# Column norms by a matmul with ones, and V taken group by group, in the attention phase of a fused kernel on one core

## The chip, the cores and the metric

The kernel runs on one core of a Trainium2 chip. The metric is the device time of one execution in microseconds (us). The kernel before takes 2712.07 us (median of 6 runs, 2706.3 to 2716.43).

## The reference

Two blocks follow each other. The first is a cross-covariance attention: the attention matrix is only 256 x 256, taken over the channels, and the sum runs over 5696 tokens. The second mixes tokens with two 5696 x 5696 matrices and channels with a 256 x 256 one. There are 4 batches.

```python
# q, k, v: (4, 5696, 256)
qn = q / (np.linalg.norm(q, axis=1, keepdims=True) + 1e-06)   # norm over the tokens, per channel
kn = k / (np.linalg.norm(k, axis=1, keepdims=True) + 1e-06)
a = softmax(kn.transpose(0, 2, 1) @ qn / tau)                 # (4, 256, 256), rows
x = v @ a
theta = x @ w_theta
zr, zi = x * np.cos(theta), x * np.sin(theta)
y = einsum('ts,bsd->btd', w_tok_r, zr) + einsum('ts,bsd->btd', w_tok_i, zi)
u = x + y
out = u + np.maximum(u @ w_ch, 0.0)
```

## The kernel before

Tokens are cut into 45 chunks of 128 rows (the last has 64), and the chunks into 12 groups of four (the last group is the 64-row chunk alone). The program has three parts. Phase 1 does the attention and the phases cos and sin for each of the 4 batches and leaves zr in SBUF, x and zi in DRAM. Pass 0 multiplies w_tok_r with zr, pass 1 w_tok_i with zi and finishes the output. The change touches phase 1 alone.

Phase 1 runs over the batches in a Python loop, and a batch has four stages, each in PSUM pools of its own that are opened and closed with the stage.

- **Stream** (L113 to L195): for each group POOL issues loads of q, k and v (qb, kb, vb; L131, L138), which turn float32 into bfloat16 on the way, into pools of two buffers. For each chunk TensorE does six matmuls of 256 columns: two halves each of G = k^T q (L149), Gq = q^T q (L156) and Gk = k^T k (L163). They add up in PSUM over the 45 chunks. Of Gq and Gk only the diagonals are used: they are the squared norms. Then TensorE transposes v (stgv, L175) and VectorE copies the result to vT (L181), which holds the whole batch.
- **Softmax** (L197 to L261): the diagonals are taken out by multiplying with an identity and adding up (L204, L213), ScalarE takes square roots (L226), VectorE adds 1e-6 and takes reciprocals (L228). The column scale is spread over the partitions by a matmul of a diagonal matrix with ones (bc_ps, L236). Then s_h (L240), the row maximum (L251), exp on ScalarE (L255), its sum's reciprocal, and a_bf (L261).
- **xT** (L263 to L281): for the whole batch, x transposed = a_bf^T vT in pieces of 512 columns (xt_ps, L274; two PSUM buffers), copied by VectorE to xT (L281).
- **E** (L283 to L376): for each group, theta (th_ps, L302) and x (x_ps, L310), each four chunks wide and with two PSUM buffers. ScalarE takes cos (L323) and sin (L326) of th_ps and copies x (L329), 1024 columns at a time; VectorE multiplies zr (L330) and zi (L336); SP stores x and zi (L366).

"The x stage" below stands for xT and E together, written x(b) for batch b, and stream(b) for its stream. The order of the work within an engine's queue is chosen by the framework's scheduler from the order of the program, the dependences and the free buffers. An engine works through its queue in order. A buffer of a pool is given out again when its last reader is done; pools that share memory or PSUM wait for each other.

Passes 0 and 1 load a row panel of the matrix (Wb, L460), transpose it on TensorE (stg, L428), copy it out (wtev, L438) and multiply it with zr or zi (acc, L571).

Of the kernel before, what the change touches and what calls it, by code (L numbers as in the profile page):

```python
# [10 lines left out]
F32 = mybir.dt.float32  # L11
# [8 lines left out]
def _csz(S: int, P: int, j: int) -> int:  # L20
    return min(P, S - j * P)
# [3 lines left out]
def kernel(  # L25
# [12 lines left out]
    nc = tc.nc  # L38
# [50 lines left out]

    with ExitStack() as ph1:  # L90
        vtp = ph1.enter_context(tc.tile_pool(name="vtp", bufs=1))
        xtp = ph1.enter_context(tc.tile_pool(name="xtp", bufs=1))
        attn = ph1.enter_context(tc.tile_pool(name="attn", bufs=1))
# [4 lines left out]
        for b in range(B):  # L98
            pair = b // 2
            bcol = (b % 2) * D  # L100

            vT = vtp.tile([P, CH, S], BF16, name="vT")
            a_bf = attn.tile([P, CH, C], BF16, name="a_bf")

            with ExitStack() as esA:
                psA = esA.enter_context(
                    tc.tile_pool(name=f"psA{b}", bufs=1, space=bass.MemoryType.PSUM)
                )
                G_ps = psA.tile([P, CH, 512], F32, name="G_ps")
                Gq_ps = psA.tile([P, CH, 512], F32, name="Gq_ps")  # L110
                Gk_ps = psA.tile([P, CH, 512], F32, name="Gk_ps")

                with ExitStack() as esB:  # L113
                    psB = esB.enter_context(
                        tc.tile_pool(name=f"psB{b}", bufs=2, space=bass.MemoryType.PSUM)
                    )
                    for g in range(NG):
                        j0 = g * GRP
                        nchunks = min(GRP, NT - j0)
                        rows0 = j0 * P  # L120
                        rows1 = min(S, rows0 + nchunks * P)
                        grows = rows1 - rows0
                        nfull = grows // P
                        tail = grows - nfull * P

                        qb = cst.tile([P, GRP, C], BF16, name="qb")
                        kb = cst.tile([P, GRP, C], BF16, name="kb")
                        vb = cst.tile([P, GRP, C], BF16, name="vb")
                        for src, dst in ((q, qb), (k, kb), (v, vb)):
                            if nfull > 0:  # L130
                                nc.gpsimd.dma_start(  # L131
                                    dst[:, 0:nfull, :],
                                    src[b, rows0:rows0 + nfull * P, :].rearrange(
                                        "(j p) c -> p j c", p=P
                                    ),
                                )
                            if tail > 0:
                                nc.gpsimd.dma_start(  # L138
                                    dst[0:tail, nfull, :],
                                    src[b, rows0 + nfull * P:rows1, :],  # L140
                                )

                        for r in range(nchunks):
                            j = j0 + r
                            csz = _csz(S, P, j)
                            first = j == 0
                            last = j == NT - 1
                            for h in range(CH):
                                nc.tensor.matmul(  # L149
                                    G_ps[:, h, 0:C],  # L150
                                    kb[0:csz, r, h * P:(h + 1) * P],
                                    qb[0:csz, r, :],
                                    start=first,
                                    stop=last,
                                )
                                nc.tensor.matmul(  # L156
                                    Gq_ps[:, h, 0:C],
                                    qb[0:csz, r, h * P:(h + 1) * P],
                                    qb[0:csz, r, :],
                                    start=first,  # L160
                                    stop=last,
                                )
                                nc.tensor.matmul(  # L163
                                    Gk_ps[:, h, 0:C],
                                    kb[0:csz, r, h * P:(h + 1) * P],
                                    kb[0:csz, r, :],
                                    start=first,
                                    stop=last,
                                )

                        for h in range(CH):
                            stgv = psB.tile([P, GRP, P], BF16, name="stgv")
                            for r in range(nchunks):
                                csz = _csz(S, P, j0 + r)
                                nc.tensor.transpose(  # L175
                                    stgv[:, r, 0:csz],
                                    vb[0:csz, r, h * P:(h + 1) * P],
                                    ident_bf[0:csz, 0:csz],
                                )
                            if tail == 0:  # L180
                                nc.vector.tensor_copy(  # L181
                                    vT[:, h, rows0:rows1],
                                    stgv[:, 0:nchunks, :].rearrange("p j n -> p (j n)"),
                                )
                            else:
                                if nfull > 0:
                                    nc.vector.tensor_copy(
                                        vT[:, h, rows0:rows0 + nfull * P],
                                        stgv[:, 0:nfull, :].rearrange("p j n -> p (j n)"),
                                    )  # L190
                                nc.vector.tensor_copy(
                                    vT[:, h, rows0 + nfull * P:rows1],
                                    stgv[:, nfull, 0:tail],
                                )

                with ExitStack() as esC:
                    psC = esC.enter_context(  # L197
                        tc.tile_pool(name=f"psC{b}", bufs=1, space=bass.MemoryType.PSUM)
                    )
                    dq = attn.tile([P, CH], F32, name="dq")  # L200
                    dk = attn.tile([P, CH], F32, name="dk")
                    scr = attn.tile([P, P], F32, name="scr")
                    for h in range(CH):
                        nc.vector.scalar_tensor_tensor(  # L204
                            out=scr,
                            in0=Gq_ps[:, h, h * P:(h + 1) * P],
                            scalar=1.0,
                            in1=ident_f32,
                            op0=MULT,
                            op1=MULT,  # L210
                            accum_out=dq[:, h:h + 1],
                        )
                        nc.vector.scalar_tensor_tensor(  # L213
                            out=scr,
                            in0=Gk_ps[:, h, h * P:(h + 1) * P],
                            scalar=1.0,
                            in1=ident_f32,
                            op0=MULT,
                            op1=MULT,
                            accum_out=dk[:, h:h + 1],  # L220
                        )
                    rq_col = attn.tile([P, CH], F32, name="rq_col")
                    rk_col = attn.tile([P, CH], F32, name="rk_col")
                    for src_c, dst_c, which in ((dq, rq_col, 0), (dk, rk_col, 1)):
                        srt = attn.tile([P, CH], F32, name="srt", tag=f"srt{which}")
                        nc.scalar.activation(srt, src_c, ACT.Sqrt)  # L226
                        nc.vector.tensor_scalar_add(srt, srt, 1e-6)
                        nc.vector.reciprocal(dst_c, srt)  # L228
# [9 lines left out]
                    for h in range(CH):  # L238
# [9 lines left out]
                        if inv_tau != 1.0:  # L248
                            nc.vector.tensor_scalar_mul(s_h, s_h, inv_tau)
# [372 lines left out]
```

## Time and profile before

| | |
|---|---|
| median of 6 runs | 2712.07 us |
| time of the profiled execution | 2714.03 us |
| its span (first to last instruction) | 2712.3 us |
| mean granted TensorE clock | 0.966 |
| TensorE busy, share of the span | 2411.6 us, 89% |
| VectorE | 598.2 us, 22% |
| ScalarE | 487.5 us, 18% |
| GpSimd (POOL) | 153.5 us, 6% |
| DMA moved | 260.89 MB, mean 96 GB/s |
| first matmul of pass 0 into acc | 503.94 us from the start |

Busy times overlap, and they are averages over parts of the program that have different limits: in the page's slices the busy share of TensorE is six to seven tenths in the first fifth of the span and nine tenths or more in most of the rest. What the change can be worth has to be read in phase 1, the first 504 us. PEld is the load of weights into TensorE; it overlaps the matmuls. The page's GB/s count what lands, that is bfloat16 bytes for the loads of q, k and v.

### The profile page before, as it was taken

Reading aid. Unit: us, or ns where it says so; the run is one execution under the profiler, and the core shown is the slowest. Engines: PE = TensorE matmul, PEld = TensorE weight load, DVE = VectorE, ACT = ScalarE, POOL = GpSimd, SP = SyncE. Lnnn points to the kernel's source line nnn. Section 1 sums busy time; section 2 is a strip of 40 time slices with the busy share of each in tenths; the row PEclk is TensorE's granted clock in tenths of the full one; section 3 lists DMA queues with packets and bytes.
Section 4 is the critical chain, followed back from the end, with each engine's and each line's share of the span. In section 5 each row is a group of like instructions: output and inputs, shape, how many; then the busy total and the mean of one; then the engine's idle time right before and its main releaser. Section 6 shows DMA issues by size and latency. Waiting matters only on the chain.

```text
span 2712.3 us, 34757 instructions
## 1 busy us (share of the span) xinstructions
PE 2411.6 (89%) x14985; PEld 1294.8 (48%) x15238; DVE 598.2 (22%) x1390; ACT 487.5 (18%) x795; POOL 153.5 (6%) x242
## 2 busy tenths in 40 slices
PE   6766676699999999999999669999999999999998
PEld 4445454344444444444444334445444444444454
DVE  2433424111111111111111102222221222222122
ACT  0505143211111111111111001111111111111111
POOL 4031220000000000000000000000000000000000
PEclk9978888899999999999999889999999999999999
DMA  9486684544444444444443454433433443344331
GB/s 154 112 112 133 85 156 83 120 89 89 89 89 88 89 88 89 88 89 88 86 84 83 109 148 99 100 79 89 100 86 84 98 100 84 84 101 99 76 92 40
DMA packets 231322, 260.89 MB, mean 96 GB/s; under 512 B 8320, under 2 KB 214144, under 8 KB 219776
## 3 DMA queue, kind: packets, MB, share of 16 engines
q0 software_dynamic: 83488, 164.79, 35.4%
q1 hardware_dynamic: 147680, 93.87, 11.3%
q8 instruction: 119, 1.95, 0.3%
q14 instruction: 35, 0.29, 0.0%
HBM read 365.07 MB, written 58.33 MB: 156 GB/s over the span
## 4 chain that ended last, share of the span: by engine, by line
PE 74%; issue 15%; DVE 4%; POOL 2%; DMA 2%; SPq 1%; ACT 1%; DVEq 0%; POOLq 0%; ACTq 0%
PE acc L571 64%; PE stg L428 8%; PE g_ps L521 2%; DVE u L497 1%; DVE utev L514 1%; POOL vb L131 1%; POOL qb L131 1%; DVE wtev L438 1%; DMA zi_dram<-zi 1%; SPq L411 1%; POOL kb L131 1%; DMA zi_res<-zi_dram 0%; DMA kb<-in_k_dram 0%; SPq L484 0%; PE xt_ps L274 0%
## 5 line engine op out<-in xcount | busy, mean ns | idle before, releaser
L571 PEld LDWEIGHTS <-wtev 128*128 128x128 bf16 (+1 forms) x8100 | 745.9, 98 | 808.8 <-issue 44.5
L571 PE MATMUL acc<-zi_res,wtev 128*128 128x512 bf16 (+2 forms) x3919 | 942.5, 380 | 45.0 <-DMA zi_res<-zi_dram 37.9
L571 PE MATMUL acc<-zr_res,wtev 128*128 128x512 bf16 (+2 forms) x3932 | 943.0, 380 | 6.8 <-DVE wtev L453 0.4
L438 ACT COPY wtev<-stg 128x512 bf16<-128x512 bf16 x440 | 257.9, 586 | 1343.8 <-PE stg L428 1296.1
L438 DVE COPY wtev<-stg 128x512 bf16<-128x512 bf16 x528 | 222.7, 422 | 1254.5 <-PE stg L428 1202.1
L428 PEld LDWEIGHTS <-Wb 128*128 128x128 bf16 (+2 forms) x4050 | 297.0, 98 | 278.8 <-issue 111.9
L428 PE MATMUL stg<-ident_bf,Wb 128*128 128x128 bf16 (+2 forms) x4050 | 389.5, 220 | 41.2 <-DVE wtev L438 22.4
L149 PE MATMUL G_ps<-qb,kb 128*128 128x256 bf16 x360 | 113.6, 315 | 65.2 <-DMA kb<-in_k_dram 55.1
L156 PE MATMUL Gq_ps<-qb 128*128 128x256 bf16 x360 | 113.1, 315 | 7.0 <-DMA qb<-in_q_dram 7.0
L478 DVE TENSOR_TENSOR up<-acc,x_in 128x512 bf16<-128x512 f32 (+1 forms) x90 | 61.7, 686 | 240.9 <-PE acc L571 240.9
L163 PE MATMUL Gk_ps<-kb 128*128 128x256 bf16 x360 | 113.1, 314 | 0.0
L497 DVE TENSOR_TENSOR u<-acc,up_in 128x512 f32<-128x512 f32 (+1 forms) x90 | 58.1, 686 | 243.4 <-PE acc L571 237.9
L302 PE MATMUL th_ps<-wth,xT 128*128 128x256 bf16 x360 | 50.9, 272 | 43.3 <-ACT sin_t L326 40.5
L521 PE MATMUL g_ps<-wch,utev 128*128 128x256 bf16 (+1 forms) x360 | 47.1, 274 | 47.3 <-DVE utev L514 47.3
L460 POOL DMA_DIRECT2D Wb<-in_moe_w_tok_i_dram x45 | 23.8, 529 | 1140.1 <-PE stg L428 1113.9
L504 ACT CAST u4b<-u 128x1024 bf16<-128x1024 f32 (+1 forms) x45 | 47.0, 1045 | 220.2 <-DVE u L497 220.2
L460 POOL DMA_DIRECT2D Wb<-in_moe_w_tok_r_dram x45 | 23.8, 530 | 1040.0 <-PE stg L428 976.7
L274 PE MATMUL xt_ps<-vT,a_bf 128*128 128x512 bf16 (+1 forms) x188 | 57.5, 404 | 25.2 <-DVE a_bf L261 16.3
L181 DVE COPY vT<-stgv 128x512 bf16<-128x512 bf16 x88 | 33.3, 420 | 197.6 <-PE stgv L175 197.6
L149 PEld LDWEIGHTS <-kb 128*128 128x128 bf16 x360 | 40.2, 112 | 70.1 <-DMA kb<-in_k_dram 60.1
L448 ACT COPY wtev<-stg 64x128 bf16<-64x128 bf16 x88 | 22.8, 259 | 282.4 <-PE stg L428 282.4
L530 DVE SCALAR_TENSOR_TENSOR or<-g_ps,u 128x256 f32<-128x256 f32 (+1 forms) x180 | 63.8, 418 | 17.4 <-PE g_ps L521 17.4
(71 smaller groups left out, 856.0 us busy)
## 6 DMA issues: line engine op xcount, KB each, us to landing
Wb<-in_moe_w_tok_r_dram POOLq DMA_DIRECT2D x44, 1424.0 KB, 10.9
Wb<-in_moe_w_tok_i_dram POOLq DMA_DIRECT2D x44, 1424.0 KB, 10.1
out_dram<-or SPq DMA_DIRECT2D x44, 512.0 KB, 4.6
qb<-in_q_dram POOLq DMA_DIRECT2D x44, 256.0 KB, 5.0
kb<-in_k_dram POOLq DMA_DIRECT2D x44, 256.0 KB, 6.0
vb<-in_v_dram POOLq DMA_DIRECT2D x44, 256.0 KB, 6.7
x_dram<-x SPq DMA_DIRECT2D x44, 256.0 KB, 2.3
zi_dram<-zi SPq DMA_DIRECT2D x44, 256.0 KB, 2.3
```

The costliest lines, as they stand in the source:

```text
L131: nc.gpsimd.dma_start(dst[:, 0:nfull, :], src[b, rows0:rows0 + nfull * P, :].rearrange("(j p) c -> p j c", p=P),)
L149: nc.tensor.matmul(G_ps[:, h, 0:C], kb[0:csz, r, h * P:(h + 1) * P], qb[0:csz, r, :], start=first, stop=last,)
L156: nc.tensor.matmul(Gq_ps[:, h, 0:C], qb[0:csz, r, h * P:(h + 1) * P], qb[0:csz, r, :], start=first, stop=last,)
L163: nc.tensor.matmul(Gk_ps[:, h, 0:C], kb[0:csz, r, h * P:(h + 1) * P], kb[0:csz, r, :], start=first, stop=last,)
L274: nc.tensor.matmul(xt_ps[:, 0:ncol], a_bf[:, h, hp * P:(hp + 1) * P], vT[:, h, t0:t0 + ncol], start=(h == 0), stop=(h == CH - 1),)
L428: nc.tensor.transpose(stg[0:ssz, r, 0:prows], Wb[0:prows, j * P:j * P + ssz], ident_bf[0:prows, 0:prows],)
L438: cp(wtev[:, 0:nchunks, :].rearrange("p j n -> p (j n)"), stg[:, 0:nchunks, :].rearrange("p j n -> p (j n)"),)
L478: nc.vector.tensor_tensor(up4[0:prows, 2 * qq:2 * qq + 2, :].rearrange("p b d -> p (b d)"), acc[qq][0:prows, :], x_in[0:prows, 2 * qq:2 * ...
L497: nc.vector.tensor_tensor(u4[0:prows, 2 * qq:2 * qq + 2, :].rearrange("p b d -> p (b d)"), acc[qq][0:prows, :], up_in[0:prows, 2 * qq:2 * ...
L521: nc.tensor.matmul(gq[bb // 2][0:prows, bb % 2, :], utev[:, bb * CH + h, 0:prows], wch[:, h, :], start=(h == 0), stop=(h == CH - 1),)
L530: nc.vector.scalar_tensor_tensor(out=or4[0:prows, bb, :], in0=gq[bb // 2][0:prows, bb % 2, :], scalar=0.0, in1=u4[0:prows, bb, :], op0=MAX ...
L571: nc.tensor.matmul(acc[qq][0:prows, :], wtev[0:ssz, r, 0:prows], zpairs[qq][0:ssz, j, :], start=(j == 0), stop=(j == NT - 1),)
```

## The change

Phase 1 is written anew as three functions that the batch loop calls one after the other: stream(b), softmax and xstage(b). All their pools are opened once for the whole phase.

- The norms: VectorE squares qb and kb into sq (bfloat16, 512 columns a chunk), and TensorE multiplies sq with a matrix of ones into nrm_ps, 512 columns wide. Every partition then holds the squared norms of all columns of q and k. Gq, Gk, the diagonal matrices and bc_ps go; ScalarE takes the root of nrm_ps's q half directly (bcq), and VectorE takes its reciprocal, now on 128 x 256 elements. The k half is still brought to one value a partition with the identity.
- stream(b) loads q and k only, with four buffers each.
- xstage(b) loads v itself, group by group (four buffers), transposes a group (stgv, now both halves in one tile, one PSUM buffer), copies it out in one step of 1024 columns, makes xT of that group (xt_ps, two PSUM buffers), and then th_ps and x_ps for two chunks at a time, with one PSUM buffer each. The steps of ScalarE and VectorE on them are 512 columns wide. vT and xT of a whole batch are no longer kept.
- PSUM: G_ps two banks, nrm_ps one, stgv one, xt_ps two, th_ps one, x_ps one.

The core of the diff:

```diff
-        vtp = ph1.enter_context(tc.tile_pool(name="vtp", bufs=1))
-        xtp = ph1.enter_context(tc.tile_pool(name="xtp", bufs=1))
-        cst = ph1.enter_context(tc.tile_pool(name="cst", bufs=2))
+        cst = ph1.enter_context(tc.tile_pool(name="cst", bufs=4))
+        vr = ph1.enter_context(tc.tile_pool(name="vr", bufs=4))
+        tg = ph1.enter_context(tc.tile_pool(name="tg", bufs=2))
...
+        psA = ph1.enter_context(tc.tile_pool(name="psA", bufs=1, space=bass.MemoryType.PSUM))
+        psX = ph1.enter_context(tc.tile_pool(name="psX", bufs=1, space=bass.MemoryType.PSUM))
+
+        def stream(b: int):
...
+                for src, dst in ((q, qb), (k, kb)):
...
+                sq = cst.tile([P, GRP, 2 * C], BF16, name="sq")
+                    nc.vector.tensor_tensor(
+                        sq[:, 0:nfull, 0:C], qb[:, 0:nfull, :], qb[:, 0:nfull, :], MULT
+                    )
...
+                    nc.tensor.matmul(
+                        nrm_ps[:, 0:2 * C],
+                        ones_bf[0:csz, :],
+                        sq[0:csz, r, :],
+                        start=first,
+                        stop=last,
+                    )
...
+        def softmax(G_ps, nrm_ps):
+            nc.scalar.activation(bcq, nrm_ps[:, 0:C], ACT.Sqrt)
...
+            nc.vector.reciprocal(bcq, bcq)
...
+        def xstage(b: int, a_bf):
...
+                vb = vr.tile([P, GRP, C], BF16, name="vb")
+                stgv = psX.tile([P, CH, GRP, P], BF16, name="stgv")
+                vT_g = tg.tile([P, CH, GRP * P], BF16, name="vT_g")
...
+                xT_g = tg.tile([P, CH, GRP * P], BF16, name="xT_g")
+                    xt_ps = psX.tile([P, GRP * P], F32, name="xt_ps", bufs=2)
...
+                for pr0 in range(0, nchunks, 2):
+                    th_ps = psX.tile([P, 2, D], F32, name="th_ps")
+                    x_ps = psX.tile([P, 2, D], F32, name="x_ps")
...
+        for b in range(B):
+            G_ps, nrm_ps = stream(b)
+            a_bf = softmax(G_ps, nrm_ps)
+            xstage(b, a_bf)
```

The order of the instructions on the engines at three places. First TensorE, in the x stage of the first batch. Before, xt of the whole batch comes first, then th and x:

```order
L274 MATMUL xt_ps<-vT,a_bf 128x64
L302 LDWEIGHTS xT
L302 MATMUL th_ps<-wth,xT 128x256
L302 LDWEIGHTS xT
L302 MATMUL th_ps<-wth,xT 128x256
L310 LDWEIGHTS vT
L310 MATMUL x_ps<-a_bf,vT 128x256
```

After, a little behind the beginning of x(0) (L153 and L160 belong to stream(1), the other lines to x(0)):

```order
L153 LDWEIGHTS kb
L153 MATMUL G_ps<-qb,kb 128x256
L160 LDWEIGHTS ones_bf
L160 MATMUL nrm_ps<-sq,ones_bf 128x512
L153 LDWEIGHTS kb
L153 MATMUL G_ps<-qb,kb 128x256
L293 LDWEIGHTS xT_g
L293 MATMUL th_ps<-wth,xT_g 128x256
L268 LDWEIGHTS a_bf
L268 MATMUL xt_ps<-vT_g,a_bf 128x512
L301 LDWEIGHTS vT_g
L301 MATMUL x_ps<-a_bf,vT_g 128x256
```

The matmuls of stream(b+1) stand between those of x(b): from the first xt of x(0) to its last th, the chunks 12 to 34 of the 45 of stream(1); the first 11 stand ahead of it, in the softmax of batch 0, and the last 11 behind it. In the steady part a pair's four th are followed by four x of the next pair, then by xt, or by transposes and one chunk of the stream.

Second VectorE, in the softmax of the first batch. Before:

```order
L213 SCALAR_TENSOR_TENSOR scr,dk<-Gk_ps,ident_f_66 128x128
L227 TENSOR_SCALAR srt<-srt 128x2 x2
L228 RECIPROCAL rq_col<-srt 128x2
L228 RECIPROCAL rk_col<-srt 128x2
L232 TENSOR_SCALAR diagm<-ident_f_66,rq_col 128x128
L237 COPY bc_sb<-bc_ps 128x128
L232 TENSOR_SCALAR diagm<-ident_f_66,rq_col 128x128
L237 COPY bc_sb<-bc_ps 128x128
L240 SCALAR_TENSOR_TENSOR s_h<-G_ps,rk_col,bc_sb 128x256 x2
```

After (sq here is that of stream(1), vT_g that of x(0)):

```order
L134 TENSOR_TENSOR sq<-qb 128x4x256
L247 COPY vT_g<-stgv 128x1024
L137 TENSOR_TENSOR sq<-kb 128x4x256
L175 SCALAR_TENSOR_TENSOR scr,dk<-nrm_ps,ident_f_66 128x128
L185 TENSOR_SCALAR bcq<-bcq 128x256
L175 SCALAR_TENSOR_TENSOR scr,dk<-nrm_ps,ident_f_66 128x128
L186 RECIPROCAL bcq<-bcq 128x256
L188 TENSOR_SCALAR dk<-dk 128x2
L247 COPY vT_g<-stgv 128x1024
L189 RECIPROCAL rk_col<-dk 128x2
L134 TENSOR_TENSOR sq<-qb 128x4x256
L193 SCALAR_TENSOR_TENSOR s_h<-G_ps,rk_col,bcq 128x256 x2
```

Squares of the next stream's groups now stand among the softmax steps: those of its first two groups ahead of the first step, those of its third and fourth ahead of s_h, exp's sum and a_bf.

Third POOL, at the end of phase 1. Before, the panels of pass 0 follow the last loads:

```order
L131 DMA qb<-in_q_dram 128x4x256
L131 DMA kb<-in_k_dram 128x4x256
L131 DMA vb<-in_v_dram 128x4x256
L138 DMA qb<-in_q_dram 64x256
L138 DMA kb<-in_k_dram 64x256
L138 DMA vb<-in_v_dram 64x256
L460 DMA Wb<-in_moe_w_tok_r_dram 128x5696 x44
```

After:

```order
L229 DMA vb<-in_v_dram 128x4x256 x4
L121 DMA qb<-in_q_dram 128x4x256
L121 DMA kb<-in_k_dram 128x4x256
L128 DMA qb<-in_q_dram 64x256
L128 DMA kb<-in_k_dram 64x256
L452 DMA Wb<-in_moe_w_tok_r_dram 128x5696
L229 DMA vb<-in_v_dram 128x4x256 x3
L452 DMA Wb<-in_moe_w_tok_r_dram 128x5696
L229 DMA vb<-in_v_dram 128x4x256 x4
L234 DMA vb<-in_v_dram 64x256
L452 DMA Wb<-in_moe_w_tok_r_dram 128x5696 x42
```

The first two panels of pass 0 are issued ahead of the last eight loads of v, and on TensorE the transposes of the first panel stand at the beginning of x(3). From the second panel on the passes hold the same instructions in the same order as before.

More of the change, by code (lines that the diff above doesn't have):

```diff
@@ L222 @@
[L222 to L228, printed above, removed]
@@ L305 @@
+                                th_ps[0:csz, rr, :],
+                                xT_g[:, h, r * P:r * P + csz],
                                 wth[:, h, :],
```

433 lines of the change are left out of this document (200 added, 233 removed).

## The prediction

> **What bounds the kernel now.** The page first: where the time lies.
>
> ```profile
> span 2712.3 us, 34757 instructions
> PE 74%; issue 15%; DVE 4%; POOL 2%; DMA 2%; SPq 1%; ACT 1%; DVEq 0%; POOLq 0%; ACTq 0%
> ```
>
> The profiled execution took 2714.0 us round this span, 2 us above the median of the runs shown (2712.07). From the first acc matmul on, TensorE is dense; the change doesn't touch that code. So the timeline: where do the stages begin?
>
> ```profile
> 8.49 0.39 PE L149 MATMUL G_ps<-qb,kb 128*128 128x256 bf16 x1 [0.63 <-DMA kb<-in_k_dram]
> 60.41 0.29 DVE L204 SCALAR_TENSOR_TENSOR scr<-Gq_ps,ident_f 128x128 f32<-128x128 f32 x1 [0.19 <-PE Gk_ps L163]
> 69.57 8.17 PE L274 MATMUL xt_ps<-vT,a_bf 128*128 128x512 bf16 x23 [4.07 <-DVE a_bf L261]
> 190.65 0.61 PE L274 MATMUL xt_ps<-vT,a_bf 128*128 128x512 bf16 x1 [4.07 <-DVE a_bf L261]
> 503.94 2.58 PE L571 MATMUL acc<-zr_res,wtev 128*128 128x512 bf16 x7 [0.22 <-issue]
> ```
>
> Phase 1 lasts 504 us: stream to 60, softmax 9 us, then the x stage, and a batch comes every 121 us (69.57 to 190.65). The stretches of the first batch (stream, softmax, xT, E), and the handover to pass 0:
>
> ```profile
> 0.00:61.00 61.00, 39.83 (x360) 32.73 (x360) 10.90 (x32) 1.28 (x1) 28.94 (x47) 0.97 1.14 153
> 61.00:70.00 9.00, 1.99 (x6) 1.27 (x8) 5.89 (x28) 2.78 (x7) 2.90 (x4) 0.56 1.27 167
> 70.00:90.00 20.00, 16.93 (x78) 7.49 (x77) 14.82 (x24) 2.94 (x3) 0.00 (x0) 0.94 0.03 4
> 90.00:123.00 33.00, 19.98 (x159) 15.56 (x157) 14.62 (x24) 32.70 (x36) 0.00 (x0) 0.96 0.54 169
> 487.00:504.00 17.00, 1.66 (x13) 1.47 (x15) 0.95 (x4) 0.59 (x1) 0.00 (x0) 0.50 0.95 213
> ```
>
> The columns are PE, PEld, DVE, ACT, POOL, granted clock, DMA share and GB/s. Each stretch has another limit: the stream the loads, xT VectorE and TensorE, E ScalarE (32.7 of 33 us), the handover the DMA queues; while one is limited the rest idle. The waits of the phase say the same:
>
> ```profile
> POOL qb L131 <- PE Gk_ps L163: 290.3, 36, 64.0
> PE G_ps L149 <- DMA kb<-in_k_dram: 55.1, 26, 4.1
> 9.00:10.00 1.00, 1.00 (x7) 0.67 (x6) 0.00 (x0) 0.00 (x0) 0.00 (x0) 1.00 1.45 196
> 13.00:14.00 1.00, 1.00 (x12) 0.90 (x10) 0.10 (x1) 0.00 (x0) 1.00 (x3) 1.00 0.56 48
> ```
>
> Loads wait up to 64 us for a buffer, a whole x stage. The full rate is 196 GB/s (at 9 us), with holes (48 GB/s at 13 us) until two buffers come free, hence 153 over the stream.
>
> **The change part by part.** The order of the instructions is given with the change: of the 45 chunks of stream(b+1) 23 now stand between the matmuls of x(b), 11 ahead of them in softmax. So a period is not a sum of stages any more, but the larger of a dependency chain and the busiest engine. The durations:
>
> ```profile
> 450.46 0.38 PE L310 MATMUL x_ps<-a_bf,vT 128*128 128x256 bf16 x2
> 450.68 0.38 PE L302 MATMUL th_ps<-wth,xT 128*128 128x256 bf16 x2
> 508.53 1.89 PE L571 MATMUL acc<-zr_res,wtev 128*128 128x512 bf16 x8
> 20.61 0.54 PEld L175 LDWEIGHTS <-vb 128*128 128x128 bf16 x8
> 459.10 1.16 ACT L323 ACTIVATE cos_t<-th_ps,pio 128x1024 bf16<-128x1024 f32 x1
> 462.00 1.19 ACT L323 ACTIVATE cos_t<-th_ps,pio 128x1024 bf16<-128x1024 f32 x1
> L438 ACT COPY wtev<-stg 128x512 bf16<-128x512 bf16 x440 | 257.9, 586 | 1343.8 <-PE stg L428 1296.1
> 456.35 0.69 DVE L330 TENSOR_TENSOR zr_res<-x,cos_t 128x1024 bf16<-128x1024 bf16 x1 [6.16 <-ACT x L329]
> 456.96 0.68 DVE L336 TENSOR_TENSOR zi<-x,sin_t 128x1024 bf16<-128x1024 bf16 x1
> 442.50 7.69 DVE L281 CAST xT<-xt_ps 128x512 bf16<-128x512 f32 x12 [0.55 <-PE xt_ps L274]
> 21.14 0.75 DVE L181 COPY vT<-stgv 128x512 bf16<-128x512 bf16 x2 [4.89 <-PE stgv L175]
> ```
>
> *TensorE.* Gq, Gk (4 matmuls of 256 columns a chunk) and the small bc matmuls go; one nrm matmul of 512 columns comes. 256 columns cost 0.107 us (two in 0.22), 512 cost 0.216 ((1.89 - 0.38)/7), a transpose 0.068 (8 in 0.54). A batch after: G 90 x 0.107 = 9.6, nrm 45 x 0.216 = 9.7, transposes 90 x 0.068 = 6.1, xt 46 x 0.216 = 9.9, th and x 180 x 0.107 = 19.3: 55 us.
>
> *ScalarE.* The ops are halved to 512 columns: three of 1024 start 2.90 us apart, 0.97 each; a 512 one lies between half of that (0.48) and the 0.586 of the copy; I take 0.54. 66.75 of them are 36 us, with softmax and table loads 42.
>
> *VectorE.* zr/zi of 1024 take 0.61 (456.35 to 456.96), of 512 between 0.31 and that: 0.37, 44 of them 16.3; casts 0.64 (7.69/12), 22 are 14; vT copies of 1024 at most two of 512, 0.75, 8.3; new: sq, 22.25 of 1024 at 0.65, 14.5; softmax some 5. Together 58 us. Of these, sq stands in the queue before the softmax steps and has to wait for its loads.
>
> *DMA.* Bytes don't change. One load (256 KB) takes 1.34 us at 196 GB/s; a batch has 33.4: 44.7 us. Its stores, 5.8 MB, move at 169 GB/s with share 0.54, so take 18.6 us of the engines. Together 63 us. Four buffers in place of two should close the holes. POOL's queue takes v loads in between now, but its issuing is no limit: 28.94 us in the first stretch for more than a batch of loads.
>
> No engine needs more than 63 us of the 121 now spent. Now the chain, with the rows of the hand-over between engines:
>
> ```profile
> 465.90 1.21 ACT L326 ACTIVATE sin_t<-th_ps,zerob 128x1024 bf16<-128x1024 f32 x1
> 467.17 1.03 PE L302 MATMUL th_ps<-wth,xT 128*128 128x256 bf16 x8 [0.99 <-ACT sin_t L326]
> L260 DVE RECIPROCAL rinv<-ssum 128x1 f32<-128x1 f32 x8 | 1.3, 164 | 0.3
> L261 DVE TENSOR_SCALAR a_bf<-e_h,rinv 128x256 bf16<-128x256 f32 x8 | 2.8, 353 | 0.3
> ```
>
> *x stage.* th_ps and x_ps have one buffer. After sin(i) ends, th starts 0.06 later (467.11 to 467.17), four matmuls end at 0.06 + 3 x 0.107 + 0.38 = 0.76, then cos and sin, 1.08: 1.9 us a pair. x_ps of the next pair and its copy lie beside that, since the order puts x(i+1) right behind th(i). With xt, transposes and one chunk of the next stream in between, TensorE closes a group of two pairs in about 3.8 us. VectorE needs per group 4 x 0.37 + 2 x 0.64 + 0.75 + 1.25 x 0.65 = 4.3 us, and so sets the pace: 11.1 groups x 4.3 = 48 us. The first casts stand behind sq of groups whose buffers come free only during softmax: 4 us more. So 52.
>
> [...]
>
> *Gap from x(b) to x(b+1).* At the end of x(b) 11 chunks remain, 11 x 0.43 = 5 us of TensorE. But sq of groups 0 to 3 of the batch after next stand in VectorE's queue before STT, s_h, ssum and a_bf. Their buffers come free only in these 5 us; eight loads and one v load at 1.34 are 12 us, then landing, two sq and the last softmax steps 4: 16 us. Were the loads there, it would be the 9 us of before; it could be 20 if landing lags. The bc round trip that goes is hidden by this wait. RECIPROCAL of 128x256 isn't in the trace: 0.16 (one column) to, say, ten times the 0.35 of the step of that shape; I take 0.35, and the dear end adds 3 us x 4.
>
> *Sum.* stream(0): the first q/k group is there at 8.5, then 23.25 loads x 1.34 = 31: 40. First xt at 40 + 16 = 56. A period is 16 + 52 = 68; four engines at 42 to 63 us in it, queues in order: I add 5 as an estimate, somewhat more than one longest wait for kb (4.1, in the waits above) in each period: 73. x(3) starts at 56 + 219 = 275. It has no stream beside it: 11.1 x 3.8 = 42, and 8 for the two Wb loads that now share the DMA with it: 50.
>
> ```profile
> 483.37 1.11 POOL L460 DMA_DIRECT2D Wb<-in_moe_w_tok_r_dram x2 [63.31 <-DVE zr_res L330]
> 486.61 11.63 SPq L373 DMA_DIRECT2D x_dram<-x  x1
> 502.46 0.28 DVE L361 TENSOR_TENSOR zi<-x,sin_t 64x256 bf16<-64x256 bf16 x1 [15.38 <-DMA zi_dram<-zi]
> ```
>
> Of the handover nearly all goes: today the Wb loads are issued at 483, block the last stores, and VectorE waits 15.4 us; after, Wb(0) is issued before the last v loads and its transposes stand in x(3). That leaves 4. First acc at about 329 instead of 504: 175 less, 2714 - 175 = 2539, say **2540**. The passes keep their instructions; I cost them at nothing, up to 5 us either way.
>
> **The rivals.** *Ping-pong.* x_ps and th_ps serialize: a pair takes 1.19 us (eight matmuls and the hand-over) + 3 x 0.54 = 2.8, 22.25 pairs 63 us; period 16 + 4 + 63 = 83, x(3) 68, first acc at 56 + 249 + 68 = 373: 2583. For it: every pair needs both engines in turn; against: the order has x a pair ahead. A stage that overlaps worse for another reason (period 85 to 100) ends at 2590 to 2640.
>
> *Down to the DMA floor.* Period 63, x(3) 44: first acc 289, 2499. For it: deeper queues; against: the gap, and VectorE's 58.
>
> *No overlap.* The stream waits for x(b) after all (no free buffers): period 16 + 52 + 40 = 108, about 2644. Against it: G_ps is free after s_h.
>
> *Half clock, slower.* The granted clock was 0.56 in softmax and 0.50 at the handover, where TensorE idled, 0.94 and 0.96 in the x stage. If the many short waits on single buffers kept it at 0.5, TensorE's 55 us become 109; at 92% use 118, with the gap a period of 134; x(3) some 77; first acc at 56 + 402 + 77 = 535, about 2745. It decides from a period of about 126 on. Against it: the E stretch has TensorE idle 40% of the time and kept 0.96.
>
> [...]
>
> **How the numbers follow.** Forecast 0.57 (2515 to 2570, periods 65 to 83), ping-pong or worse overlap 0.24 (2570 to 2640), DMA floor 0.10 (2495 to 2515), no overlap 0.04, half clock 0.03, and 0.02 that other losses bring it to 2714 and nothing shows. I leave out half of the floor case and what lies above 2610 (0.06 of the second, and the last three): range 2505 to 2610. Within 0.2% (5 us, about what a measurement of this kernel tells from no change) 0.02, slower 0.03, faster 0.95.
>
> **What would show it.** In the profile after: the first xt at 50 to 62 us; G and th matmuls in the same slices; first acc at 300 to 355; VectorE the busiest of the small engines at 75% or more in the x stage; VectorE waiting for qb or kb loads in softmax; clock above 0.85 in the x stage; no stretch like 487 to 504. Wrong, if th waits for sin more than 1.5 us a pair (ping-pong), if periods are above 95, or if the passes change by more than 10 us.

## The result, and the profile after

The changed kernel takes 2543.52 us (median of 8 runs, 2536.73 to 2547.15), beside 2712.9 us for the kernel before (median of 16 runs): a ratio of 0.9371, 95% interval 0.9355 to 0.9387. The forecast was 2540, the range 2505 to 2610. The profiled execution took 2539.84 us round a span of 2538.0. The top of the page, and the chain of waits by engine:

```profile
span 2538.0 us, 33903 instructions
PE 80%; issue 8%; DMA 4%; DVE 4%; POOL 2%; SPq 1%; ACT 1%; DVEq 0%; POOLq 0%; ACTq 0%
```

In the chain, "issue" fell from 15% of the span to 8% and TensorE rose from 74% to 80%: empty stretches went. TensorE's busy time fell too, from 2411.6 to 2340.7 us; what the smaller work is worth alone, e1 shows below. The timeline of TensorE shows where each x stage begins (its first xt matmul), and the first acc of pass 0:

```profile
56.87 0.60 PE L268 MATMUL xt_ps<-vT_g,a_bf 128*128 128x512 bf16 x2 [1.16 <-DVE ssum L209]
128.82 0.61 PE L268 MATMUL xt_ps<-vT_g,a_bf 128*128 128x512 bf16 x2 [1.25 <-DVE ssum L209]
204.43 0.61 PE L268 MATMUL xt_ps<-vT_g,a_bf 128*128 128x512 bf16 x2 [2.43 <-DVE ssum L209]
279.50 0.63 PE L268 MATMUL xt_ps<-vT_g,a_bf 128*128 128x512 bf16 x1 [0.53 <-DVE ssum L209]
328.65 1.92 PE L563 MATMUL acc<-zr_res,wtev 128*128 128x512 bf16 x4 [0.98 <-ACT sin_t L337]
```

Periods are 72.0, 75.6 and 75.1 us where they were 121, 124 and 118; the first acc is at 328.65 instead of 503.94, 175.3 us earlier. From there to the end of the span it is 2209.3 us, before 2208.4: the passes changed by 1 us. All of the gain lies ahead of the first acc.

Cut at the end of the last sin of each batch, the same timelines give x stages and gaps. The means are over batches 0 to 2, x(3) stands alone, "handover" is from the last sin to the first acc, all in us:

| kernel | first xt | x stage | gap | x(3) | handover | first acc |
|---|---|---|---|---|---|---|
| before | 69.6 | 52.7 | 68.4 | 53.3 | 17.8 | 503.9 |
| after | 56.9 | 53.2 | 21.0 | 49.1 | 0.1 | 328.7 |

The x stage kept its length, though it now also transposes v and carries half of the next stream. The gain is three times 47.4 us of gap (142), 12.7 ahead of the first xt, 17.8 of handover, and 2.5 in the four x stages: 175. By stretches, for x(0), its gap, x(1), its gap, and x(3); the columns are PE, PEld, DVE, ACT and POOL busy, granted clock, DMA share and GB/s:

```profile
56.90:108.20 51.30, 47.84 (x361) 31.99 (x369) 42.40 (x91) 40.92 (x70) 15.02 (x21) 1.00 1.20 206
108.20:128.80 20.60, 15.00 (x86) 8.67 (x85) 13.78 (x36) 4.38 (x9) 11.23 (x15) 0.75 1.37 196
128.80:181.40 52.60, 47.87 (x361) 32.09 (x369) 42.75 (x92) 41.00 (x70) 15.01 (x21) 1.00 1.16 201
181.40:204.40 23.00, 13.93 (x86) 7.88 (x84) 14.03 (x36) 4.37 (x9) 11.19 (x15) 0.85 1.32 185
279.50:328.60 49.10, 38.67 (x301) 26.85 (x305) 37.14 (x83) 41.38 (x71) 3.50 (x5) 0.98 0.79 178
```

In x(0) TensorE is busy for 93% of the time, VectorE for 83%, ScalarE for 80%; before, in E, ScalarE was busy for 99% and TensorE for 61%. In the gap ScalarE has 4 of 21 us.

What the gap waits for stands in VectorE's timeline, in its order:

```profile
109.85 0.69 DVE L134 TENSOR_TENSOR sq<-qb 128x1024 bf16<-128x1024 bf16 x1 [4.04 <-DMA qb<-in_q_dram]
112.34 0.69 DVE L137 TENSOR_TENSOR sq<-kb 128x1024 bf16<-128x1024 bf16 x1 [1.46 <-DMA kb<-in_k_dram]
119.42 0.29 DVE L185 TENSOR_SCALAR bcq<-bcq 128x256 f32<-128x256 f32 x1
119.62 0.28 DVE L175 SCALAR_TENSOR_TENSOR scr<-nrm_ps,ident_f 128x128 f32<-128x128 f32 x1
119.83 1.75 DVE L186 RECIPROCAL bcq<-bcq 128x256 f32<-128x256 f32 x1
121.50 0.10 DVE L188 TENSOR_SCALAR dk<-dk 128x2 f32<-128x2 f32 x1
127.42 0.69 DVE L137 TENSOR_TENSOR sq<-kb 128x1024 bf16<-128x1024 bf16 x1 [1.80 <-DMA kb<-in_k_dram]
128.41 0.35 DVE L212 TENSOR_SCALAR a_bf<-e_h,rinv 128x256 bf16<-128x256 f32 x1
```

The first two rows are squares of stream(1)'s last full group, whose loads are late; the rows in between are softmax; the sq at 127.42 belongs to the stream after next and waits 1.80 us just ahead of a_bf, as the prediction has it. Why the first loads are late stands in the timelines of TensorE and POOL. Loads of q and k take the buffers of the group four before theirs, and these come free with that group's last G matmul:

```profile
102.03 0.28 PE L153 MATMUL G_ps<-qb,kb 128*128 128x256 bf16 x1
102.41 0.74 POOL L229 DMA_DIRECT2D vb<-in_v_dram  x1 [2.24 <-PE G_ps L153]
103.14 0.75 POOL L121 DMA_DIRECT2D qb<-in_q_dram  x1
```

The first row is the last G matmul of group 6 of stream(1) (groups counted from 0). POOL waits for it, then issues a load of v and the load of q for group 10. So four buffers, and an order that puts these matmuls late in the x stage, hold the loads back; the load of v ahead of them costs 0.7 us.

The third gap is hardly shorter (19.3 us), though no further stream follows whose squares could stand in it. There the first panel of pass 0 takes their place:

```profile
277.25 1.71 PE L420 MATMUL stg<-ident_bf,Wb 128*128 128x128 bf16 x12 [5.16 <-DMA Wb<-in_moe_w_tok_r_dram]
277.90 0.42 DVE L430 COPY wtev<-stg 128x512 bf16<-128x512 bf16 x1 [5.17 <-PE stg L420]
278.24 0.14 DVE L205 TENSOR_SCALAR m_h<-m_h 128x1 f32<-128x1 f32 x1
```

The panel's first copy stands in VectorE's queue ahead of a softmax step (m_h) and waits 5.17 us for the panel. Its transposes stand ahead of the first xt of x(3), not inside x(3). (The second panel's load stands ahead of the last five loads of v, the first ahead of the last eight.) So a part of the handover is still there, in another place.

In the x stage, ScalarE's timeline gives the pace of the pairs, here three pairs in 5.97 us, 1.99 each:

```profile
85.14 0.69 ACT L309 ACTIVATE cos_t<-th_ps,pio 128x512 bf16<-128x512 f32 x1 [0.34 <-PE th_ps L293]
91.11 0.69 ACT L309 ACTIVATE cos_t<-th_ps,pio 128x512 bf16<-128x512 f32 x1 [0.27 <-PE th_ps L293]
```

Nearly all pairs keep this pace: of the 22 spacings from sin to sin in x(0), 17 lie between 1.95 and 2.09 us, in x(3) 20.

### The profile page after: what moved, and what is told of

Same layout as the page of the kernel before. It is cut to its first block, busy times and chain, and to the rows that moved or that the text cites. A ratio compares the mean times of both kernels' runs of the same rounds, so it can differ in the third digit from the quotient of the medians.

```text
span 2538.0 us, 33903 instructions
## 1 busy us (share of the span) xinstructions
PE 2340.7 (92%) x14403; PEld 1223.6 (48%) x14682; DVE 651.8 (26%) x1500; ACT 514.9 (20%) x927; POOL 153.7 (6%) x242
## 4 chain that ended last, share of the span: by engine, by line
PE 80%; issue 8%; DMA 4%; DVE 4%; POOL 2%; SPq 1%; ACT 1%; DVEq 0%; POOLq 0%; ACTq 0%
PE acc L563 68%; PE stg L420 8%; PE g_ps L513 2%; DMA qb<-in_q_dram 1%; DVE u L489 1%; DVE utev L506 1%; DVE wtev L430 1%; POOL vb L229 1%; DMA kb<-in_k_dram 1%; SPq L403 1%; PE th_ps L293 1%; DMA x_dram<-x 1%; POOL kb L121 1%; DMA zi_res<-zi_dram 1%; PE xt_ps L268 0%
## 5 line engine op out<-in xcount | busy, mean ns | idle before, releaser
L563 PEld LDWEIGHTS <-wtev 128*128 128x128 bf16 (+1 forms) x8100 | 746.8, 98 | 811.7 <-issue 48.5
L153 PE MATMUL G_ps<-qb,kb 128*128 128x256 bf16 x360 | 73.2, 289 | 23.8 <-DMA kb<-in_k_dram 22.1
L293 PE MATMUL th_ps<-wth,xT_g 128*128 128x256 bf16 x360 | 56.2, 273 | 16.2 <-ACT sin_t L312 8.5
L160 PE MATMUL nrm_ps<-sq,ones_bf 128*128 128x512 bf16 (+1 forms) x158 | 64.4, 425 | 5.8 <-DVE sq L137 3.0
L309 ACT ACTIVATE cos_t<-th_ps,pio 128x512 bf16<-128x512 f32 x88 | 60.5, 688 | 23.2 <-PE th_ps L293 23.2
L275 DVE CAST xT_g<-xt_ps 128x512 bf16<-128x512 f32 (+1 forms) x96 | 61.2, 648 | 6.0 <-PE xt_ps L268 5.1
L301 PE MATMUL x_ps<-a_bf,vT_g 128*128 128x256 bf16 x360 | 56.1, 273 | 5.0 <-ACT x L315 4.8
L312 ACT ACTIVATE sin_t<-th_ps,zerob 128x512 bf16<-128x512 f32 x88 | 59.9, 681 | 0.0
```

Source lines behind the costliest of these rows:

```text
L153: nc.tensor.matmul(G_ps[:, h, 0:C], kb[0:csz, r, h * P:(h + 1) * P], qb[0:csz, r, :], start=first, stop=last,)
L160: nc.tensor.matmul(nrm_ps[:, 0:2 * C], ones_bf[0:csz, :], sq[0:csz, r, :], start=first, stop=last,)
L275: nc.vector.tensor_copy(xT_g[:, hp, 0:grows], xt_ps[:, 0:grows])
L293: nc.tensor.matmul(th_ps[0:csz, rr, :], xT_g[:, h, r * P:r * P + csz], wth[:, h, :], start=(h == 0), stop=(h == CH - 1),)
L309: nc.scalar.activation(cos_t[:, pr0:pr0 + 2, :], th_ps, ACT.Sin, bias=pio2, scale=1.0)
L563: nc.tensor.matmul(acc[qq][0:prows, :], wtev[0:ssz, r, 0:prows], zpairs[qq][0:ssz, j, :], start=(j == 0), stop=(j == NT - 1),)
```

## The experiments

Two questions: which part of the change gives how much, and whether the reasons of the prediction hold, namely VectorE as the pace of the x stage (theory) against the loop between TensorE and ScalarE or the DMAs (rivals), and loads that come late as the cause of the gap. The stages of all kernels, from their timelines as above:

| kernel | first xt | x stage | gap | x(3) | first acc | ratio to before, 95% interval |
|---|---|---|---|---|---|---|
| e1_norms_only | 69.0 | 53.7 | 59.6 | 54.1 | 481.0 | 0.9944 [0.9923, 0.9966] |
| e2_before_bufs4 | 62.0 | 53.2 | 48.0 | 53.7 | 437.0 | 0.9779 [0.9759, 0.9799] |
| e3_no_overlap | 55.4 | 51.0 | 39.9 | 54.2 | 383.5 | 0.9571 [0.9546, 0.9596] |
| after | 56.9 | 53.2 | 21.0 | 49.1 | 328.7 | 0.9371 [0.9355, 0.9387] |
| e8_v_once | 55.6 | 52.3 | 19.0 | 49.8 | 319.2 | 0.9342 [0.9322, 0.9363] |
| e4_bufs7 | 61.2 | 54.5 | 19.5 | 49.1 | 332.4 | 0.9378 [0.9361, 0.9395] |
| e9_vr8 | 64.1 | 56.1 | 20.6 | 48.9 | 343.2 | 0.9409 [0.9378, 0.9441] |
| e10_vr8_cst6 | 63.0 | 56.2 | 19.2 | 49.3 | 338.5 | 0.9396 [0.937, 0.9422] |
| e6_th_two | 57.5 | 60.7 | 20.4 | 47.2 | 348.5 | 0.9443 [0.9426, 0.946] |
| e7_vt_act | 58.4 | 65.8 | 11.9 | 54.5 | 346.0 | 0.9436 [0.9418, 0.9454] |
| e11_no_cos | 57.4 | 61.4 | 19.9 | 47.4 | 348.6 | 0.9437 [0.9413, 0.946] |
| e12_sq_once | 57.1 | 56.6 | 18.1 | 49.6 | 331.0 | 0.9353 [0.9323, 0.9383] |
| e13_grp4 | 56.5 | 53.1 | 21.3 | 48.5 | 328.4 | 0.9361 [0.9335, 0.9386] |

An edit moves more than it names, since the order of the queues is made anew for each kernel; the rows have to tell what came of it.

**The parts of the change**

*e1: the kernel before with the new norms alone.*

```
-  Gq_ps, Gk_ps (4 matmuls of 256 columns a chunk), bc by matmuls
+  sq = qb*qb, kb*kb;  nrm_ps += ones_bf^T sq (one matmul of 512 columns)
```

> The kernel before with the norms by the ones matmul alone (sq, nrm; no Gq, Gk, bc), all else as before. Theory (the gain is the overlap of stages that had different limits, and the closed holes of the loads): the stream stays bound by loads into two buffers, so TensorE's 14 us a batch less buy little: 2690 to 2720 us. Rival (the gain is the smaller work of TensorE): some 14 us for each of four batches, 2655 us or less.

Measured: 2694.25 us, theory. The first acc is 23 us earlier; the three gaps, between stages that still stand one behind the other, give 26 of it, the x stages take 4 back, and the handover stays (18.0 us). So the smaller work of TensorE, the rival, is worth little in the kernel before.

*e2: the kernel before with four buffers.*

```
-  cst = ... tile_pool(name="cst", bufs=2)
+  cst = ... tile_pool(name="cst", bufs=4)
```

> The kernel before with four buffers of qb, kb and vb in place of two, nothing else. Theory: holes in the loads close in the first stream (60 to about 50 us), and four groups instead of two are loaded during the x stage, so later streams fall towards TensorE's 36 us: 2620 to 2650 us, less than half of the gain is left to the overlap. Rival (the gain is the overlap alone): 2700 us or more.

Measured: 2650.33 us, just above the dear end of theory. One number in one line brings the first acc 67 of the 175 us forward: q, k and v of four groups are there when the x stage ends, and the gap falls by 20 us. That is under half; 108 us are left to the rest of the change, and e3 tells how much of them is the overlap.

*e3: the new kernel, but no matmul of stream(b+1) before x(b) has ended.*

```
-  psA, psX opened once for all batches
+  for each b:  psA (G_ps, nrm_ps) opened and closed, then psX in the same banks
```

> The kernel after, but the PSUM of the stream and of the x stage are the same banks, so that no matmul of stream(b+1) can run before x(b) is done; loads and squares still run ahead by four buffers. Theory: the x stage alone takes 44 us (VectorE without the squares), then some 24 us of stream, then 10 of softmax: a period of 80 instead of 74, 2560 to 2580 us. The document's price for no overlap (period 108) says 2640; a theory in which overlap of matmuls is nearly the whole gain says 2620 or more.

Measured: 2593.38 us, above theory and below the document's price. Theory had 44 us for an x stage without the squares beside it; it took 51.0. The stretches of its x(0) and the gap behind it:

```profile
55.40:106.30 50.90, 40.15 (x302) 27.26 (x303) 37.77 (x84) 40.85 (x70) 7.97 (x11) 0.96 0.90 166
106.30:145.10 38.80, 24.18 (x151) 14.01 (x151) 20.68 (x45) 4.37 (x9) 18.16 (x25) 0.91 1.18 160
```

Against the new kernel's x(0), TensorE has 7.7 and VectorE 4.6 us less to do in the stage, and the stage is as long (50.9 to 51.3; 51.0 to 53.2 on average): what the overlap adds to an x stage is nearly free, and neither TensorE's 93% nor VectorE's 83% sets the stage's length. The overlap shortens the gap from 38.8 to 20.6. The overlap of matmuls is worth 54.9 us of first acc; the other 120 come without it, from buffers, norms and v by groups. The handover is 1.2 us here, 18.0 in e1 and 17.6 in e2, so it does not go with the overlap; v by groups, which puts loads of v behind the first panels in POOL's queue, is the likely cause, but no run has it alone.

**What bounds a period**

*e8: one load of v a batch.*

```
-  vb = vr.tile(...); dma_start(vb, v[b, rows of g])      for every g
+  if g == 0: vb = vr.tile(...); dma_start(vb, v[b, rows of group 0])
```

> The kernel after, with v loaded once a batch (the first group, used for all groups, so the output is that of another v): 10 loads of 33 a batch go, 14 us of DMA time at full rate. Theory (the period is the dependency chain of gap and x stage, DMA is not the bound): one load less in each gap, 2530 to 2543 us. Rival (phase 1 now sits on the DMA floor): 10 us or more for each batch, 2500 us or less.

Measured: 2531.64 us, theory. The bandwidth of the loads is not the floor of a period. In the view of the DMA queues from 57 to 129 us the new kernel shows for the loads

```profile
q0 software_dynamic: 17607, 8.72, 94.9%
```

and e8 from 56 to 128 us

```profile
q0 software_dynamic: 12258, 6.08, 66.3%
```

(packets, MB, share of 16 engines). Three tenths of the bytes and of the queue's time go, and the periods fall from 72.0, 75.6 and 75.1 us to 70.8, 71.4 and 71.6 only, 9 us in all three.

*e4, e9, e10: more buffers.*

```
e4    cst bufs 4 -> 7
e9    vr  bufs 4 -> 8
e10   cst bufs 4 -> 6, vr bufs 4 -> 8
```

> The kernel after with seven buffers of qb, kb and sq in place of four. Theory (the gap between x stages, 21 us, is made by squares in VectorE's queue that wait for loads whose buffers come free late): the gap falls to about 12, the period from 74 to 66, 2515 to 2525 us. Rival (DMA bounds the whole period): the gap shrinks and the x stage grows, 2535 to 2545 us.

> The new kernel with 8 instead of 4 buffers for v (q/k stay at 4). In the new kernel's trace the last q/k loads of a stream are issued only as the x stage ends (102 to 111 us in the first), because POOL's queue is in order and v loads ahead of them wait 3 to 4.5 us each for stgv, that is for a v buffer. Theory A (these v waits in POOL's queue hold the q/k loads back, and so make the gap 21 us instead of 16): with 8 buffers the q/k loads come earlier until their own 4 buffers hold them; gaps 15 to 18, time 2525 to 2535. Rival B (POOL would wait for q/k buffers at the same place anyway, or the x stage gives it back): gaps 19 to 23, time 2538 to 2548.

> The new kernel with 8 v buffers and 6 q/k/sq buffers in place of 4 and 4. Theory A (in-order POOL queue: both kinds of wait must go before the stream can run ahead): the stream ends before the x stage does, the gap falls to the softmax chain alone, 11 to 14 us, time 2505 to 2520. Rival B (the scheduler puts the same chunks behind the x stage, or the transfers come in the x stage's way, so that it grows as with 7 q/k buffers): gap 15 to 22 or x stage 55 to 58, time 2535 to 2550.

Measured: 2543.26, 2551.76 and 2547.86 us. The rival in e4 (whose reason, the DMAs, fell with e8) and B in e10; e9 is above both of its ranges. In sum more buffers gain nothing, but the gaps tell two cases apart. In the third gap, which no further stream follows, e4 and e10 have 15.9 and 15.1 us against 19.3, and last periods of 67.1 and 68.6 against 75.1 (x(2) is shorter there too): the stream's own last squares no longer wait there, as e4's theory has it. (e9, with more buffers for v alone, has 19.5.) In the first two gaps squares of the stream after next use up what was won. VectorE's timelines behind x(0), of e9 and of e10:

```profile
126.26 0.69 DVE L134 TENSOR_TENSOR sq<-qb 128x1024 bf16<-128x1024 bf16 x1 [5.40 <-DMA qb<-in_q_dram]
```

```profile
121.60 0.69 DVE L134 TENSOR_TENSOR sq<-qb 128x1024 bf16<-128x1024 bf16 x1 [1.52 <-DMA qb<-in_q_dram]
125.50 0.69 DVE L137 TENSOR_TENSOR sq<-kb 128x1024 bf16<-128x1024 bf16 x1 [3.02 <-DMA kb<-in_k_dram]
```

All three belong to stream(2), and wait for loads ahead of the softmax steps of batch 1; in e4 and e10 squares of five of its groups stand in this gap instead of four. The first x stage, too, begins 4 to 7 us later (at 61 to 64 us instead of 57). In e4 more squares of stream(1) stand among the softmax steps before it; in e9 and e10 more loads of v go ahead of those of q and k, and the first square of stream(1) waits 3.55 and 8.27 us instead of 2.08. The queue's order uses the buffers up.

*e12: the squares of the first group only.*

```
-  sq of every group
+  if g == 0: sq = ...     (used by the nrm matmuls of all groups)
```

> The new kernel with the squares made for the first group of a batch alone; its nrm matmuls use that tile for all groups (the norms are then other numbers). VectorE loses 20 of 22 large sq operations a batch, 0.6 us each, 12 us, and with them the waits for loads that stand in its queue ahead of the softmax steps and of the last zr and zi; loads, matmuls and ScalarE stay. Theory A (these squares cost twice, in the pace of the x stage and in the gap, as predicted): x stage 46 to 49 us instead of 51 to 55, gap 14 to 17 instead of 19 to 23; time 2505 to 2522. Theory C (gap alone: the x stage goes at the loop between TensorE and ScalarE): stage 50 to 53, gap 14 to 17; time 2520 to 2532. Rival B (neither: TensorE's own waits for the late loads set the gap): 2535 to 2548.

Measured: 2538.43 us, rival B by the time (5 us below the new kernel, the intervals overlap). Its x(0) and gap, by stretches, and two places of its gap on VectorE, with the end of it on TensorE:

```profile
57.10:113.00 55.90, 48.34 (x359) 32.65 (x364) 37.24 (x80) 40.85 (x70) 15.11 (x23) 0.97 1.15 193
113.00:131.40 18.40, 14.09 (x91) 8.34 (x90) 8.20 (x25) 4.25 (x8) 10.28 (x14) 0.81 1.39 209
```

```profile
118.59 0.69 DVE L134 TENSOR_TENSOR sq<-qb 128x1024 bf16<-128x1024 bf16 x1 [2.86 <-DMA qb<-in_q_dram]
119.93 0.69 DVE L137 TENSOR_TENSOR sq<-kb 128x1024 bf16<-128x1024 bf16 x1 [0.65 <-DMA kb<-in_k_dram]
127.52 0.35 DVE L205 TENSOR_SCALAR a_bf<-e_h,rinv 128x256 bf16<-128x256 f32 x1
127.91 2.78 PE L146 MATMUL G_ps<-qb,kb 128*128 128x256 bf16 x24
131.06 0.50 PE L146 MATMUL G_ps<-qb,kb 128*128 128x256 bf16 x3 [0.36 <-DMA kb<-in_k_dram]
131.39 0.59 PE L261 MATMUL xt_ps<-vT_g,a_bf 128*128 128x512 bf16 x2
```

VectorE is down to 67% of the x stage, and the stage is longer, not shorter: VectorE does not set its pace. (Why it is longer, the runs do not tell.) And the gap hardly shrinks. The squares that e12 keeps, of stream(2)'s first group, still wait 2.86 and 0.65 us ahead of the first softmax step; so e12 does not show what a gap without any square would be. And a_bf is ready at 127.87, but 27 G matmuls of the next stream stand ahead of xt on TensorE and cost 3.5 us: a part of the wait moved from VectorE's queue to TensorE's.

**What sets the pace of the x stage**

*e7: the vT_g copies of full groups on ScalarE.*

```
-  nc.vector.tensor_copy(vT_g, stgv)
+  nc.scalar.copy(vT_g, stgv)
```

> The kernel after with the copy of the transposed v (11 of 1024 columns a batch) on ScalarE instead of VectorE. Theory (VectorE sets the pace of the x stage): VectorE loses 7 us a batch there, ScalarE has room: 2515 to 2530 us. Rival (the loop of TensorE and ScalarE sets it): ScalarE's 1 us a group lies in that loop, 2550 to 2575 us.

Measured: 2558.4 us, rival.

```profile
58.40:123.20 64.80, 51.34 (x392) 34.74 (x396) 41.73 (x91) 51.36 (x82) 22.88 (x32) 0.97 1.20 197
123.20:136.00 12.80, 8.51 (x54) 5.07 (x57) 7.79 (x25) 5.78 (x10) 2.75 (x4) 0.76 0.84 126
```

ScalarE gets 10.4 us more, and the stage grows by 13.5: what is added to ScalarE costs at once. More of the stream now fits beside it, so the gap falls to 12.8, about the softmax steps alone; the sum of the two is what counts, and here it is 77.6 us, 5.6 more.

*e6: two buffers for th_ps (both halves of G_ps in one bank to make room).*

```
-  G_ps = psA.tile([P, CH, 512]);  th_ps = psX.tile([P, 2, D])
+  G_ps = psA.tile([P, CH, C]);    th_ps = psX.tile([P, 2, D], bufs=2)
```

> The kernel after with both halves of G in one PSUM bank and the bank that this frees as a second buffer of th_ps. Theory (VectorE sets the pace of the x stage): 0 to 10 us less, 2533 to 2543 us. Rival (the ping-pong of TensorE and ScalarE on one buffer sets it): a pair falls from 1.98 to about 1.7 us, some 6 us a batch, 2515 to 2525 us.

*e11: no cos in full pairs.*

```
-  nc.scalar.activation(cos_t, th_ps, Sin, bias=pio2);  zr = x4 * cos_t
+                                                       zr = x4 * sin_t
```

> The new kernel without the cos of full pairs (zr is x times sin instead): ScalarE has two operations a pair instead of three, VectorE, TensorE and the DMAs keep all theirs. Theory A (the x stage goes at the pace of the loop th, cos, sin, th between TensorE and ScalarE, 1.98 us a pair): the loop falls to about 1.4 us, the stage to VectorE's 42 to 43 us of work plus its fill, 44 to 47 us instead of 51 to 53; time 2510 to 2525. Rival B (VectorE sets the pace, as predicted): the stage stays at 50 to 53 us, time 2533 to 2545.

Measured: 2560.49 and 2557.86 us, outside both theories, on the slow side. Both speed up the loop: in e6 the pairs come 1.61 us apart where nothing else holds them, and x(3), which has no stream beside it, falls from 49.1 to 47.2 and 47.4. ScalarE's timeline of e6:

```profile
67.31 0.74 ACT L309 ACTIVATE cos_t<-th_ps,pio 128x512 bf16<-128x512 f32 x1
68.92 0.77 ACT L309 ACTIVATE cos_t<-th_ps,pio 128x512 bf16<-128x512 f32 x1
```

The three stages with a stream beside them get about 8 us longer. Near the end of x(0), on VectorE and TensorE of e6:

```profile
106.43 0.69 DVE L134 TENSOR_TENSOR sq<-qb 128x1024 bf16<-128x1024 bf16 x1 [3.57 <-DMA qb<-in_q_dram]
109.03 0.39 PE L293 MATMUL th_ps<-wth,xT_g 128*128 128x256 bf16 x1 [3.99 <-DVE xT_g L275]
```

and of e11:

```profile
101.66 0.69 DVE L134 TENSOR_TENSOR sq<-qb 128x1024 bf16<-128x1024 bf16 x1 [3.76 <-DMA qb<-in_q_dram]
105.91 0.40 PE L293 MATMUL th_ps<-wth,xT_g 128*128 128x256 bf16 x1 [5.05 <-DVE xT_g L275]
```

A faster loop runs into squares whose loads have not landed; the casts xT_g stand behind them in VectorE's queue, and th behind the casts. In the new kernel's x stages the longest wait of a square is 1.8 us.

*e13: four buffers for the stored tiles.*

```
-  grp = ... tile_pool(name="grp", bufs=2)
+  grp = ... tile_pool(name="grp", bufs=4)
```

> The new kernel with 4 instead of 2 buffers for x4 and zi4, the tiles that are stored. In the new kernel's x stages ScalarE's copy x waits seven times for x_dram<-x, 6.9 us, and x_dram lands 5.0 us after its issue against 2.3 before. Theory A (these waits lie on the loop of the x stage): 5 to 9 us less in all, 2532 to 2539. Rival B (the loop has slack there, or VectorE is next): within 3 us of the new kernel, 2540 to 2547.

Measured: 2539.18 us, between the two numbers; the ratio can't be told from that of the new kernel. First acc 328.4, as before the edit: rival B by the trace. The waits for stores are not free everywhere, though. In x(2) of the new kernel, its longest stage, a copy of ScalarE waits for a buffer that is being stored:

```profile
232.80 0.59 ACT L315 CAST x<-x_ps 128x512 bf16<-128x512 f32 x1 [3.71 <-DMA x_dram<-x]
```

The two spacings of pairs there are 5.45 and 3.75 us instead of 2.0. In e13 these waits are gone and x(2) falls from 55.8 to 53.1, but x(0) rises from 51.3 to 53.3, and the mean stays at 53.

No variant that computes the reference is faster than the new kernel by more than the runs can tell.

## Why the prediction was right

The sum was 56 + 3 x 73 + 50 + 4 = 329; measured are 56.9 + 222.6 + 49.1 + 0.1 = 328.7. That the four terms differ by +0.9, +3.6, -0.9 and -3.9 and add up to nearly nothing is luck in part:

- *stream(0) and the first xt* (56): 56.87. Right, with a RECIPROCAL dearer by 1.4 us in it.
- *Gap* (16): 20.6, 23.0 and 19.3. In the first two the mechanism is there: squares of the batch after next, waiting for loads, ahead of the softmax steps. The size was off by 5, and two waits were left out. The last full group's own loads come late, since their buffers come free only with late G matmuls (its first square waits 4.04, 6.47 and 4.78 us); and in the third gap, without any square of a later batch, the first panel of pass 0 is waited for. "Its issuing is no limit" holds for POOL, busy for 15.0 of 51.3 us in x(0) and 11.2 of 20.6 in the gap behind it. RECIPROCAL of 128x256 takes 1.75 us, five times the value taken and half of the dear end, 1.4 more.
- *Allowance* (5): the 5 of the gap came out of it. It had the right size for a reason it did not name.
- *x stage* (52): 51.3, 52.6 and 55.8. The number holds, the reason does not. That VectorE "sets the pace" with 4.3 us a group fell with e3 and e12, and its 42.4 us of work in x(0) are 3.8 a group. The pace is that of the loop between TensorE and ScalarE, which the prediction had worked out and then passed over: 1.99 us a pair (1.9 forecast), 44 us for 22.25 pairs, with 4.5 us from the first xt to the first sin ahead of them and single delays besides. e7, which lengthens the loop, costs at once. Shortening it gains little, because other limits lie close behind: in x(3) of e6 pairs at 1.61 us could save 22 x 0.38 = 8.4 us, and 1.9 came. Beside a stream the late squares cost more than that (e6, e11). Which limit comes next in x(3) is not separated.
- *x(3) and handover* (50 + 4): 49.1 + 0.1. The stretch like 487 to 504 is gone, but not all of the handover: 5.2 us of waiting for the first panel stand in the third gap. So the -3.9 here is no saving; it is paid ahead of x(3), within the periods and their +3.6.
- *Passes* (0): 1.0 us.

Of the rivals, ping-pong did not come: its sign was th waiting for sin over 1.5 us a pair, and the waits from 57 to 329 us show

```profile
PE th_ps L293 <- ACT sin_t L312: 8.5, 14, 1.0
ACT cos_t L309 <- PE th_ps L293: 23.2, 78, 2.0
```

8.5 us in all, the longest 1.0. ScalarE's 23.2 us over 78 waits, 0.3 each, is about what one buffer of th_ps costs in the loop (0.38 a pair by e6). In x(3) that second buffer gained 1.9 us in all; in the stages with a stream beside them the same edit lost 7.5 us each, so for the time of this kernel the measurement decides against it.

The DMA floor is refuted by e8, with the queue 95% taken as it is. The price of no overlap was mis-sized: 108 us a period and 2644, against 91 (the mean of three) and 2593 in e3, since four groups of loads and squares go ahead of the x stage's end even then; the rival counted the whole stream. Half clock did not come: the granted clock is 1.00 in x(0) and x(1), where the longest wait of a matmul for another engine is 1.5 us, and 0.75 and 0.85 in the gaps, where softmax before showed 0.56.

## What to carry to other kernels

Before predicting an overlap, cut the timeline into stages and gaps: here the x stages kept their length and most of the gain was gap (142 of 175 us); a deeper pool alone (one number) gave 67 of the 175. In in-order queues, look for work of a later stage that waits for a load ahead of work that is due: here the squares of a later batch in two gaps (1.80 and 2.15 us in the last wait of each) and the first panel of pass 0 in the third (5.17 us). Freeing an engine or a buffer moved such a wait to other work or another queue more often than it removed it. Where two or three limits lie close together, a right total does not show which of them is the limit; taking work from each, and the spacing of the repeated steps, does.

## What the runs showed of the hardware

The reciprocal of a 128x256 tile in f32 takes 8.4 times as long as a TENSOR_SCALAR of its shape: the next instruction starts 1.67 us behind it (119.83 to 121.50), 0.20 behind a TENSOR_SCALAR (119.42 to 119.62). In the list of issues the median time from issue to landing of the stores of x rose from 2.3 us before, where in the first batch next to no loads went on beside them (0.07 MB from 70 to 123 us), to 5.0. Before:

```profile
x_dram<-x SPq DMA_DIRECT2D x44, 256.0 KB, 2.3
```

and after:

```profile
x_dram<-x SPq DMA_DIRECT2D x44, 256.0 KB, 5.0
zi_dram<-zi SPq DMA_DIRECT2D x44, 256.0 KB, 4.4
```

In the first period, where e8 loads three tenths fewer bytes, the stores of x take 3.6 us in e8 and 5.3 in the new kernel.
